# One hand-written step order exchanged for another in a DeltaNet and feed-forward kernel

## The chip, the cores and the metric

The kernel runs on one NeuronCore of one Trainium2 chip. Five engines work from queues of their own: TensorE (PE; its weight loads are shown as PEld), VectorE (DVE), ScalarE (ACT), GpSimd (POOL) and SyncE (SP, which here only issues DMAs). Each executes its own instructions in order, and semaphores tie the queues together. Matrix products are written to PSUM, everything else lies in SBUF. The metric is the device time of one launch in microseconds, the median of a few runs. A profiled execution has its own time and its own span, from the first instruction to the last.

## The reference

Two parts, one after the other. The first is a delta rule over 768 time steps, for 4 batches and 8 heads of size 48; the second is a feed-forward block on its 3072 output rows.

```python
k_n = k / (norm(k) + 1e-6)
for t in range(S):
    y[t] = q[t] @ state
    v_old = state.T @ k_n[t]
    state = state + beta[t] * outer(k_n[t], v[t] - v_old)
x = y as (3072, 384)
out = ((x @ w1) * (x @ w2)) @ w3 @ w_out
```

The weights arrive as float64, w1 and w2 as 384 x 1024, w3 as 1024 x 1024, w_out as 1024 x 384.

## The kernel before, in words

The sequence is cut into 12 chunks of 64 time steps. Inside a chunk the recurrence becomes small matrix products and the inverse of a triangular matrix; the state goes from chunk to chunk. Two chunks at a time share one inverse (V0 to V5) and one block of the feed-forward part (512 columns, u = 0 to 5). The product w3 @ w_out is folded into one matrix at the start.

Every piece of work is a Python generator that emits some instructions between two `yield`s. The string `ORDER` (line 39) names generators; a name's next occurrence runs the generator to its next `yield`. Each engine executes its instructions in the order in which the string emitted them (`in_text_order`, at the end). So the string is the whole schedule: it sets which PE phase follows which, and what stands ahead of what on DVE, ACT, POOL and SP. The framework adds semaphores where data or buffers demand them. Buffers rotate in the order of the calls: two PSUM tiles `ps_w` for the small phases (one while V0 or V1 holds the other), four `ps_f` banks, five `raw` tiles for arriving weights.

The names, with the PE lines that tell them in the profile:

- `k`, `q`, `v`, `p`: loads of a chunk (`p` is the permuted load, 8 DMAs for k and 8 for q; chunks 0 and 1 use `K`, `Q`, PE transposes of L337, instead). `d`: four DVE transposes of what `p` loaded.
- `g`, `N`: squares (POOL), sums (DVE) and the inverse norms of two chunks (14 DVE operations), each with a small PE exchange (L255).
- `P0` to `P35`: a piece of a weight: DMA on SP, two ACT operations (L710, L713), one DVE (L715), one POOL (L717). 0 to 7 are w_out, 8 to 23 w3, 24 to 29 w1, 30 to 35 w2. `t`: transposes of w3 (L752). `f`: half a fold twice (L761), then its copy (L768). `T`: four sums of the folded weight (POOL).
- `s`: scores of a chunk, two PE phases (L367, L373), evacuated by DVE (L379, L397; ACT and POOL for the first two chunks). `u`: four DMAs that store the score blocks in DRAM.
- `V`: the substitution: a load of the blocks (L426), 31 pairs of DVE operations (L440, L445), a store (L453). `V0` and `V1` work in PSUM, with ACT copies ahead (L434) and behind (L449).
- `e`: joins the inverse of a chunk: eight DMAs, one DVE transpose (L481), two PE phases (L498) with an ACT copy after each (L514, L525).
- `n`: two POOL products on v. `c`: the chunk's chain, up to three PE phases (L551): the old values from the state (DVE R, L585), the new values X (L597), the next state S (L616, L618).
- `y`: the chunk's output, one PE phase of 128 matmul records (64 for chunk 0) with a drain between two modes (L655), eight ACT copies to `xT` (L676), and six DMAs.
- `a`, `b`: x @ w1 and x @ w2 for 128 columns, each 6 matmul records (L781), with an ACT copy (L793) and a DVE product (L797). `a25` is block 2, columns of group 5; `b` is the first half of block 0. `S`: 16 POOL sums of their results (L848). `o`: seven PE phases of 16 records against the folded weight (L876). `x`: the output sums (ACT, DVE) and their stores.

The text calls `a`, `b`, `o` and `f` phases dense (full 128 x 128 tiles), the others small.

## Time and profile before

| | us |
|---|---|
| median of 3 runs | 606.77 (606.45 to 607.84) |
| profiled execution | 609.02 |
| its span, first to last instruction | 607.2 |
| PE busy in the span | 554.8 |
| mean granted TensorE clock | 0.943 of full speed |

The page shows one profiled execution. Its second part cuts the span into 40 slices of some 15 us; a digit is the busy share in tenths, PEclk the granted TensorE clock in tenths. The chain of waits goes back from the last instruction to what released it at each step; "issue" is time in which an engine waited for nothing that the profile shows. The busy time by stretch gives, per engine, busy us and the number of instructions, then the granted clock, the DMA share and the rate. A matmul of float32 stands in the trace as two records, each with its weight load.

### The profile page before, as it was taken

What the parts mean: (1) busy time and instruction counts of PE and PEld (TensorE: products, weight loads), DVE (VectorE), ACT (ScalarE), POOL (GpSimd) and SP (SyncE); (2) the same over time, 40 slices, a digit from 0 to 9 for tenths busy, and PEclk for the clock granted to TensorE, in tenths of its full rate; (3) what the DMA queues carried; (4) which work ended last, traced back from release to release, by engine and by line L of the source; (5) the groups of instructions that cost most, each with busy time, mean ns of one, the idle gap of its engine ahead of it and who ended that gap; (6) DMA issues with size and microseconds to landing.
All of it is one profiled execution on the core that took longest, in us unless ns stands there. A gap on an engine that the chain in (4) does not pass through costs nothing.

```text
span 607.2 us, 18976 instructions
## 1 busy us (share of the span) xinstructions
PE 554.8 (91%) x8188; PEld 387.3 (64%) x8188; DVE 334.0 (55%) x792; ACT 159.2 (26%) x333; POOL 175.2 (29%) x223
## 2 busy tenths in 40 slices
PE   4558997869998999999899998999899999999997
PEld 4444655658887864469844587644687446874477
DVE  2551886538975369665597555793464863310112
...
PEclk9657999759999999999899999999899999999999
...
GB/s 193 172 225 271 202 78 164 152 131 143 144 111 72 98 90 100 87 89 76 56 105 74 98 60 77 104 114 79 27 46 78 45 71 18 17 41 13 1 0 52
DMA packets 219506, 57.30 MB, mean 94 GB/s; under 512 B 206656, under 2 KB 212800, under 8 KB 219424
## 3 DMA queue, kind: packets, MB, share of 16 engines
...
q8 instruction: 64, 1.05, 0.8%
q14 instruction: 18, 0.15, 0.1%
...
## 4 chain that ended last, share of the span: by engine, by line
PE 83%; issue 6%; DVE 4%; ACT 3%; DMA 2%; POOL 1%; ACTq 0%; SPq 0%; DVEq 0%; POOLq 0%
PE ps_f L781 41%; PE ps_f L876 19%; PE ps_w L551 5%; PE ps_f L761 5%; PE ps_w L655 4%; PE ps_w L498 2%; PE ps_w L367 2%; PE ps_w L373 2%; PE ps_f L752 1%; DMA ktok<-in_k_dram 1%; PE ps_w L876 1%; POOL w L717 1%; DMA raw<-in_moe_w_out_dram 1%; ACT raw L713 1%; DMA TT<-Vd 1%
## 5 line engine op out<-in xcount | busy, mean ns | idle before, releaser
L781 PE MATMUL ps_f<-xT,w2s 128*128 128x512 f32 (+1 forms) x336 | 131.5, 536 | 0.3 <-issue 0.3
L781 PE MATMUL ps_f<-xT,w1s 128*128 128x512 f32 (+1 forms) x336 | 130.1, 537 | 0.0
L848 POOL TENSOR_TENSOR ab<-ab 128x256 f32<-128x256 f32 x96 | 67.0, 728 | 192.1 <-DVE ab L797 181.9
L781 PEld LDWEIGHTS ps_f<-xT,w1s 128*128 128x128 f32 x336 | 64.4, 193 | 55.7 <-issue 51.2
L781 PEld LDWEIGHTS ps_f<-xT,w2s 128*128 128x128 f32 x336 | 62.6, 190 | 55.7 <-issue 52.2
L793 ACT COPY ab<-ps_f 128x512 f32<-128x512 f32 (+1 forms) x56 | 28.6, 524 | 178.1 <-PE ps_f L781 178.1
L876 PE MATMUL ps_f<-w,ab 128*128 128x192 f32 x376 | 68.6, 336 | 1.2 <-issue 0.7
L797 DVE TENSOR_TENSOR ab<-ab,ps_f 128x512 f32<-128x512 f32 (+1 forms) x56 | 33.4, 604 | 64.2 <-PE ps_f L781 64.1
L876 PEld LDWEIGHTS ps_f<-w,ab 128*128 128x128 f32 x376 | 62.5, 194 | 4.5 <-issue 3.4
L676 ACT COPY xT<-ps_w 48x256 f32<-48x256 f32 x96 | 30.5, 365 | 84.2 <-PE ps_w L655 83.7
L876 PE MATMUL ps_f<-room,ab 128*128 128x192 f32 x272 | 50.4, 339 | 1.1 <-DVE room L907 0.8
L761 PE MATMUL ps_f<-w2s,w3T 128*128 128x384 f32 x128 | 46.7, 523 | 1.7 <-ACT w3T L755 1.7
L445 DVE TENSOR_TENSOR Vb<-Vb,tb 128x31 f32<-128x31 f32 (+15 forms) x124 | 45.0, 363 | 4.3
L440 DVE TENSOR_TENSOR tb<-Vb,Ub 128x31 f32<-128x31 f32 (+15 forms) x124 | 44.4, 358 | 5.2 <-DMA Ub<-Ud 1.6
L876 PEld LDWEIGHTS ps_f<-room,ab 128*128 128x128 f32 x272 | 45.6, 196 | 2.4 <-issue 1.6
L270 POOL TENSOR_TENSOR sq<-ktok 128x384 f32<-128x384 f32 x24 | 19.9, 844 | 78.3 <-DMA qperm<-in_q_dram 29.8
L537 POOL TENSOR_TENSOR vtok<-vtok,n 128x384 f32<-128x384 f32 x24 | 20.0, 849 | 65.3 <-DMA vtok<-in_v_dram 30.3
L761 PEld LDWEIGHTS ps_f<-w2s,w3T 128*128 128x128 f32 x128 | 25.7, 206 | 19.8 <-issue 3.3
L379 DVE TENSOR_TENSOR U<-ps_w,wt 128x512 f32<-128x512 f32 x24 | 16.5, 689 | 36.2 <-PE ps_w L373 36.1
L367 PE MATMUL ps_w<-KQ 48*64 48x128 f32 x384 | 30.2, 302 | 6.7 <-DVE KQ L349 4.3
L717 POOL TENSOR_TENSOR w<-w,raw 128x512 uint32<-128x512 uint32 x16 | 20.9, 1316 | 43.9 <-ACT raw L713 15.4
L373 PE MATMUL ps_w<-KQ 48*64 48x64 f32 x768 | 31.3, 239 | 1.6 <-issue 1.6
...
## 6 DMA issues: line engine op xcount, KB each, us to landing
...
```

The lines of the kernel that those rows point to most:

```text
L367: pe.matmul(ps[half(z), 0, n : n + 128], lhsT=x[:, 0, :], rhs=x.rearrange("p j t -> p (j t)"), start=True, stop=True,)
L373: pe.matmul(ps[half(z ^ j), 1, n + C * j : n + C * j + C], lhsT=x[:, 0, :], rhs=x[:, j, :], start=True, stop=True,)
L440: dve.tensor_tensor(out=tv, in0=V[:, 0 : s + 1, s : s + 1].to_broadcast([P, s + 1, n]), in1=U[:, s, s + 1 : BS].unsqueeze(1).to_broadcast( ...
L445: dve.tensor_tensor(out=o, in0=o, in1=tv, op=ALU.subtract)
L551: pe.matmul(out(ps, r, h, z), lhsT=lhs(r, h, z), rhs=rhs(r, h, z), start=True, stop=True,)
L676: act.copy(out=xT[f, p:NP:2, b : b + NR, cc, :].rearrange("p a r t -> p r a t"), in_=pyv[f, z, b : b + NR],)
L761: pe.matmul(ps[:, 0:DM], lhsT=w3Ts[jc, kc // 4][:, kc % 4 * P : kc % 4 * P + P], rhs=wo[:, kc], start=(kc == 0), stop=(kc == KF - 1),)
L781: pe.matmul(ps[:].rearrange("p b c t -> p b (c t)"), lhsT=w[:, m, js], rhs=x[:, m, :, c0:c1].rearrange("p b c t -> p b (c t)"), start=(m = ...
L793: act.copy(out=t, in_=ps)
L797: dve.tensor_tensor(out=t, in0=t, in1=ps, op=ALU.mult)
L848: pool.tensor_tensor(out=o_, in0=x_, in1=y_, op=op)
L876: pe.matmul(ps[b][:, b, :], lhsT=abs_[u, HF * f + i][:, t0 : t0 + P], rhs=ws_[w][:, i], start=first and i == 0 and (b == 0 or n == "F"), s ...
```

## The change

Only the string `ORDER` is replaced. Both strings hold 1317 entries, and each name occurs equally often in both, so every instruction is the same; their order on each engine differs, and with it the rotation of the buffers. In the PE order the new string puts dense phases (`o`, `a`, `b`) at other places between the small ones. Around chunks 7 to 9, for example, PE goes from

```
before: ... c7 o2 c7 y7 o2 c8 o2 a31 ...   a37 e9 y8 o3 s10 s10 o3 c8 e9 o3 s11 s11 c9 o3 c9 y9 o3 c9
after:  ... c7 o2 y7 o2 c7 o2 a33 ...      a36 y8 s10 o3 e9 s10 o3 c8 e9 o3 c9 s11 s11 c9 o3 y9 o3 c9
```

The diff, cut: the start, and the rows around chunks 4 to 5 and 7 to 9.

```diff
-V0 beta q1 beta beta k0 K0 K0 K0 K0 K0 Q1 g0 g0 q0 Q1 Q1 k1 g0 g0 K1 K1 Q1 K1 Q1 g0 g0 g0 g0 g0
-g0 N0 K1 P10 P10 K1 s1 N0 P10 P13 Q0 P13 P9 P10 t2 P13 P13 P0 P9 P0 N0 P9 P12 P12 P12 P12 P0 P0
-p2 P9 t1 Q0 Q0 d2 P15 d2 k2 P11 t5 Q0 Q0 P15 s0 P15 P15 s0 s0 s1 s1 s0 s0 s0 s1 s1 s1 g1 t7 g1
-g1 g1 P11 P11 P11 P8 P8 P8 P8 P14 P14 P14 P18 P18 P18 t1 t2 t4 P14 t6 P18 t5 P4 P4 P3 P3 P3 t10
-P1 P3 s0 P4 P4 P1 P1 P1 t6 t7 t3 t4 P2 P2 u0 P2 P2 t0 t0 f2 P5 P5 P5 P6 P6 P6 P6 t10 f0 u1 P5 P7
-P7 P7 P7 f2 f2 P19 t3 f1 f1 V0 P19 P19 P19 V0 V0 V0 V0 V0 V0 V0 V0 V0 V0 V0 s1 s1 f0 P17 t11 f3
-t11 f3 v0 V0 P17 P17 P17 P20 P20 f0 V0 V0 t9 P20 P20 f1 t12 t12 V0 V0 V0 V0 P16 P16 V0 V0 P16
-P22 P22 P22 f3 P22 t9 f5 f5 t14 P16 t8 t8 f4 f4 V0 V0 p2 d2 f5 t14 f7 V0 d2 P23 P23 V0 V0 V0 V0
-V0 V0 V0 V0 V0 V0 V0 V0 P23 P23 t15 t15 f4 k3 g1 g1 g1 g1 g1 g1 N1 p3 d3 P21 P21 P21 n0 f6 p3 f7
-f7 V0 P31 e0 e0 P21 N1 N1 e0 P31 P31 P31 s2 e0 n0 t13 e0 e0 d3 t13 P25 s2 s2 c0 c0 P25 P25 s2 s2
-s2 e1 s0 y0 y0 P24 c0 f6 v1 n1 P25 e1 V1 n1 e1 e1 P32 P24 c0 d3 d3 s3 s3 s3 s3 s3 s3 c1 c1 P26
-u2 e1 e1 c1 P26 P26 P30 P26 f6 P30 P30 P30 c1 y1 y0 u3 P32 P32 y1 P24 P28 V1 c1 c1 V1 V1 V1 V1
-P32 V1 V1 V1 V1 V1 V1 P24 b1 b0 b2 b2 b1 V1 V1 P34 b0 b0 b3 b3 b0 V1 y1 a02 P28 P28 a02 a02 a00
-P33 P33 a02 V1 P27 V1 V1 a01 a00 P28 P27 P27 P27 a01 a01 c2 a00 V1 V1 P29 P29 P29 P29 V1 V1 b5
-a05 a01 P34 P34 P34 a03 a00 V1 V1 V1 V1 p4 a06 V1 P33 b5 P33 a03 P35 P35 P35 a05 b7 V1 V1 V1 b7
-b4 b4 a06 P35 V1 a03 V1 V1 V1 V1 v2 n2 n2 b6 b6 a03 k5 k4 g2 b6 b6 c2 d4 d4 g2 p4 g2 a05 a05 g2
-a06 V1 g2 a07 V1 V1 d4 d4 a07 b2 b2 a04 a04 T a06 b3 g2 b3 b1 b1 g2 g2 T a04 a07 T e2 e2 a04 g2
-a07 v3 n3 T e3 e2 e2 b7 e2 s4 e2 c2 n3 g2 N2 s4 b5 s4 s4 b4 c2 s4 y2 y2 b4 s4 p5 p5 c2 c2 o0 b5
...
-g3 d6 g3 N2 g3 N3 e4 a16 p7 c4 c4 s6 s6 e5 s6 a17 v6 n6 y4 s6 s6 s6 a16 y4 o1 e5 x1 e5 e5 S1 c4
-a17 o1 S1 S1 d7 d7 u6 d7 d7 s7 S1 S1 S1 S1 S1 S1 n6 n5 n5 c4 s7 s7 s7 s7 u7 s7 o1 x1 x1 S1 S1 S1
-S1 e5 e5 c5 o1 V3 c5 c5 c5 V3 V3 V3 o1 c5 p8 y5 y5 y5 x1 o1 V3 V3 V3 V3 c5 c6 x1 x1 S1 o1 x1 V3
...
-o2 S2 S2 S2 c6 x2 S2 s9 s9 s9 s9 s9 s9 v8 u9 o2 S2 S2 n7 V4 n7 e7 e7 c7 o2 x2 n8 n8 c7 c7 c7 x2
-V4 o2 V4 V4 V4 V4 c7 c7 V4 V4 y7 o2 c8 x2 c8 S2 V4 S2 v9 o2 x2 y7 y7 a31 k11 x2 x2 x2 S2 S2 V4
...
-g5 c8 a37 c8 g5 N5 a36 S3 d10 d10 e9 e9 a37 S3 y8 y8 o3 S3 S3 S3 S3 s10 x3 p11 d11 s10 s10 V5
-s10 o3 S3 S3 S3 S3 s10 s10 d11 p11 u10 c8 e9 e9 d11 d11 c8 o3 S3 S3 S3 S3 x3 x3 s11 s11 s11 s11
-s11 u11 c9 o3 s11 n9 c9 c9 c9 y9 o3 x3 c9 V5 V5 V5 V5 V5 V5 o3 y9 y9 a44 x3 x3 o3 x3 a44 x3 x3
...
+V0 beta k0 q0 beta beta K0 K0 K0 P14 P14 K0 Q0 g0 k1 g0 g0 g0 g0 g0 g0 g0 g0 g0 Q0 P14 Q0 K0 Q0
+Q0 K1 P9 s0 P9 P14 N0 N0 P9 K1 K1 K1 K1 q1 Q1 N0 P9 t1 P10 P10 P10 P10 P15 P15 t2 Q1 Q1 Q1 t6 Q1
+P11 P11 P15 s1 P15 t7 P8 P8 P11 P8 P11 P8 s0 P13 s0 P13 s0 s0 s1 P18 P18 P18 t1 t2 t3 t0 P12 P12
+t3 P0 s1 t7 t6 P18 t10 P13 P13 t5 P0 P12 P12 s1 s1 t5 P0 P0 t0 p2 d2 t4 P1 s0 s0 P1 P1 s1 d2 P3
+P2 P1 P2 P2 P2 P3 P3 P6 P3 f0 P6 P4 P6 P6 u0 t10 u1 P5 f1 f3 P7 V0 V0 s1 s1 P4 P4 P5 P5 P4 P5 P7
+P7 P7 f0 f0 t4 f3 V0 V0 V0 f1 f2 f2 V0 V0 V0 k2 g1 V0 V0 f3 V0 V0 P22 P22 P16 v0 n0 P16 V0 V0
+P19 P19 P22 P22 t14 f1 V0 V0 V0 V0 P19 P19 t11 V0 V0 V0 P16 f2 t14 t11 V0 V0 V0 f5 P16 n0 P17 f5
+V0 P17 P17 V0 t8 V0 V0 P17 t9 P23 P23 P23 P23 t8 f4 V0 V0 V0 V0 P20 V0 V0 P20 P20 P20 f5 t9 t15
+f4 f7 p3 d3 d3 P21 P21 P21 P21 V0 V0 t12 p2 f4 d2 d2 t15 f7 P25 t12 f6 V0 k3 e0 e0 e0 e0 g1 g1
+g1 g1 g1 g1 g1 g1 g1 N1 f7 e0 e0 t13 t13 v1 P25 P25 P25 s2 N1 c0 N1 s2 s2 s2 c0 P29 s0 y0 P29 s2
+s2 c0 c0 y0 f6 e1 e1 c1 e1 n1 n1 c1 e1 e1 P24 P24 p3 d3 d3 s3 e1 c1 P29 V1 P29 P30 P30 P30 P26
+P26 P31 P31 s3 s3 s3 f6 u2 P32 P32 P30 P24 P24 y0 c1 y1 y1 s3 s3 u3 P26 P26 b3 b3 P31 b1 b1 P32
+P32 P31 c1 c1 P27 b1 V1 V1 b1 P27 P27 P27 V1 V1 V1 V1 b2 b2 b0 b0 b0 V1 V1 y1 a00 a02 V1 c2 b0
+P28 V1 P28 P28 P28 b4 b4 a00 V1 V1 V1 V1 V1 b6 k4 g2 P35 P35 P34 b6 V1 V1 V1 V1 a02 P34 b7 b7
+a02 a02 P33 V1 V1 p4 P33 P34 a05 a03 a03 V1 V1 V1 V1 V1 V1 P34 b5 b5 a07 a05 a04 a04 k5 V1 V1
+P35 a07 P35 a01 a01 a01 V1 V1 V1 V1 v2 V1 p4 a01 V1 V1 V1 e2 a06 a06 P33 P33 a03 g2 a03 a00 a00
+g2 g2 d4 g2 b3 b3 a07 d4 d4 g2 g2 a04 a07 a04 p5 a06 b4 a05 a06 g2 g2 n2 n2 c2 e2 e2 e2 b2 g2
+a05 e2 T T V2 d4 b4 b6 v3 n3 e2 c2 b7 s4 N2 c2 y2 y2 e3 s4 b5 b7 s4 s4 b6 b2 o0 s4 x0 s4 c2 e3
+S0 e3 T e3 p5 T b5 o0 c2 e3 S0 S0 S0 d5 u4 S0 d5 S0 d5 c3 d5 n3 c3 o0 e3 s5 s5 S0 s5 p6 s5 o0 s5
...
+e4 e5 s6 e4 g3 N3 s6 s6 a13 a13 a14 c4 N3 N2 a13 p7 a14 S1 S1 S1 S1 n5 o1 v6 x1 N2 c4 y4 p7 d7
+d7 d7 e5 p8 o1 y4 e5 e5 c4 c4 N3 o1 e5 d7 p8 S1 S1 S1 c5 s6 o1 s6 s6 S1 S1 S1 S1 S1 u6 n5 c5 s7
+s7 x1 s7 s7 S1 S1 s7 s7 x1 c5 o1 c5 c5 y5 n6 x1 o1 y5 c5 c6 u7 V3 y5 V3 V3 x1 x1 S1 S1 o1 x1 x1
...
+a26 e6 c6 g4 s8 a25 a25 n7 N4 N4 c6 y6 y6 v8 s8 s8 o2 a25 a26 S2 S2 S2 S2 S2 c6 S2 e7 e7 S2 p9
+o2 d9 S2 S2 S2 d9 S2 c6 c7 e7 e7 c7 N4 p9 d9 x2 o2 S2 S2 s8 S2 e7 S2 d9 s9 o2 s9 v9 n9 V4 n9 s8
+u8 s8 s9 s9 c7 s9 s9 x2 o2 c7 y7 x2 x2 o2 u9 x2 x2 V4 V4 c7 o2 y7 y7 a33 a33 V4 V4 x2 x2 x2 V4
...
+d10 a30 a30 a33 k11 a35 g5 g5 a35 a35 e8 e8 e8 e8 p11 c8 a33 e9 S3 a32 e8 a37 g5 a35 e8 S3 g5 g5
+g5 d10 c8 c8 c8 a36 y8 y8 e9 g5 a32 s10 o3 p11 e9 e9 N5 a37 s10 V5 s10 s10 d11 a36 o3 S3 s10 s10
+c8 d11 d11 d11 S3 S3 S3 e9 S3 S3 S3 x3 o3 u10 e9 c8 c9 c9 s11 s11 s11 s11 s11 s11 S3 c9 S3 o3 x3
+c9 y9 x3 o3 x3 u11 V5 V5 V5 V5 y9 V5 c9 V5 V5 V5 y9 S3 o3 a45 x3 x3 S3 S3 S3 S3 o3 x3 V5 x3 x3
```

More of the change, by code (lines that the diff above doesn't have):

```diff
@@ L58 @@
-c3 e3 e3 b7 o0 d5 d5 p6 x0 S0 c3 S0 u4 S0 e3 e3 e3 S0 d5 d5 s5 o0 x0 S0 S0 S0 V2 c3 s5 S0 s5 s5
-s5 c3 v4 S0 u5 s5 o0 o0 x0 V2 c3 y3 S0 S0 y3 n4 x0 S0 o0 c3 y3 S0 S0 S0 S0 x0 x0 x0 V2 V2 c4 V2
-V2 p6 x0 V2 o0 V2 x0 x0 x0 a14 a14 a14 V2 V2 V2 V2 V2 a14 V2 V2 V2 a15 a17 V2 V2 a17 V2 V2 V2 V2
-V2 a15 a15 V2 k6 V2 k7 V2 a13 a15 a11 a11 a13 V2 V2 V2 V2 V2 V2 a10 V2 a12 a12 a10 a10 d6 a10 S1
-d6 d6 a13 a13 v5 g3 g3 g3 n4 g3 c4 V2 a12 a12 g3 e4 g3 a11 e4 e4 N2 a11 S1 e4 a16 a16 e4 p7 g3
-g3 d6 g3 N2 g3 N3 e4 a16 p7 c4 c4 s6 s6 e5 s6 a17 v6 n6 y4 s6 s6 s6 a16 y4 o1 e5 x1 e5 e5 S1 c4
@@ L64 @@
-a17 o1 S1 S1 d7 d7 u6 d7 d7 s7 S1 S1 S1 S1 S1 S1 n6 n5 n5 c4 s7 s7 s7 s7 u7 s7 o1 x1 x1 S1 S1 S1
-S1 e5 e5 c5 o1 V3 c5 c5 c5 V3 V3 V3 o1 c5 p8 y5 y5 y5 x1 o1 V3 V3 V3 V3 c5 c6 x1 x1 S1 o1 x1 V3
-V3 x1 V3 V3 V3 a20 a20 k8 x1 x1 x1 a22 a22 c6 a23 a23 a25 a25 V3 V3 V3 V3 V3 V3 V3 V3 V3 V3 V3
-V3 a21 V3 k9 V3 V3 V3 V3 V3 V3 V3 a21 a26 a26 a26 a26 a25 a25 a23 a23 g4 p8 g4 g4 g4 g4 d8 d8
-a24 a22 a24 a24 g4 g4 V3 d8 g4 d8 a22 e6 e6 g4 e6 e6 g4 N4 N3 V4 a24 a20 p9 p9 e7 s8 e6 e6 a21
-v7 s8 s8 s8 s8 c6 s8 a20 S2 e7 u8 a27 a27 N3 c6 y6 a27 d9 d9 d9 d9 e7 a21 y6 S2 a27 S2 S2 c6 e7
@@ L70 @@
-o2 S2 S2 S2 c6 x2 S2 s9 s9 s9 s9 s9 s9 v8 u9 o2 S2 S2 n7 V4 n7 e7 e7 c7 o2 x2 n8 n8 c7 c7 c7 x2
-V4 o2 V4 V4 V4 V4 c7 c7 V4 V4 y7 o2 c8 x2 c8 S2 V4 S2 v9 o2 x2 y7 y7 a31 k11 x2 x2 x2 S2 S2 V4
-S2 S2 p10 o2 V4 V4 v11 x2 x2 x2 a31 V4 V4 V4 V4 V4 V4 d10 V4 a37 a30 V4 V4 V4 V4 V4 a30 V4 a37
-a33 V4 a33 V4 V4 k10 g5 g5 a36 p10 a36 V4 V4 V4 a34 a33 a33 a32 V4 V4 g5 g5 g5 g5 a31 a31 g5 g5
-a34 a34 e8 a32 a34 e8 a35 a35 a35 a32 a35 d10 n9 e8 a30 N4 N4 a30 S3 S3 a32 e8 e8 e9 e8 e9 a36
-g5 c8 a37 c8 g5 N5 a36 S3 d10 d10 e9 e9 a37 S3 y8 y8 o3 S3 S3 S3 S3 s10 x3 p11 d11 s10 s10 V5
@@ L76 @@
-s10 o3 S3 S3 S3 S3 s10 s10 d11 p11 u10 c8 e9 e9 d11 d11 c8 o3 S3 S3 S3 S3 x3 x3 s11 s11 s11 s11
-s11 u11 c9 o3 s11 n9 c9 c9 c9 y9 o3 x3 c9 V5 V5 V5 V5 V5 V5 o3 y9 y9 a44 x3 x3 o3 x3 a44 x3 x3
-V5 V5 V5 V5 x3 a40 a40 x3 a43 a46 a43 a46 a42 a42 a42 V5 V5 V5 V5 n11 n11 V5 V5 V5 V5 V5 V5 V5
-V5 V5 V5 V5 V5 V5 V5 V5 a42 a40 a45 V5 V5 V5 a40 a45 a41 a41 a44 a44 a43 a43 v10 a46 n10 a47 V5
-e10 c9 e10 e10 e10 a41 a41 N5 a46 c10 N5 e10 o4 a47 n10 c10 e10 c10 a45 c10 y10 y10 a47 c10 e11
-e11 e11 a45 a47 e11 o4 c10 c11 c11 e11 x4 o4 e11 c11 x4 x4 S4 S4 S4 S4 o4 S4 S4 S4 S4 S4 S4 S4
@@ L82 @@
-c11 y11 o4 x4 S4 o4 x4 y11 S4 S4 S4 S4 x4 y11 a52 a52 x4 x4 x4 o4 x4 a56 a56 a55 a57 a55 a57 a55
-a55 a54 a54 a52 a52 x4 a54 a50 a50 a50 a54 a50 S5 a51 a56 a56 a51 a51 a51 S5 S5 a57 a53 a57 a53
-a53 a53 S5 o5 S5 S5 S5 S5 x5 o5 S5 S5 S5 S5 o5 S5 S5 S5 S5 x5 o5 x5 o5 x5 o5 x5 x5 x5 o5 x5 x5
-x5 x5 x5 x5 x5
+V0 beta k0 q0 beta beta K0 K0 K0 P14 P14 K0 Q0 g0 k1 g0 g0 g0 g0 g0 g0 g0 g0 g0 Q0 P14 Q0 K0 Q0
+Q0 K1 P9 s0 P9 P14 N0 N0 P9 K1 K1 K1 K1 q1 Q1 N0 P9 t1 P10 P10 P10 P10 P15 P15 t2 Q1 Q1 Q1 t6 Q1
@@ new lines @@
+a02 a02 P33 V1 V1 p4 P33 P34 a05 a03 a03 V1 V1 V1 V1 V1 V1 P34 b5 b5 a07 a05 a04 a04 k5 V1 V1
[3 more added lines that the diff above has]
+S0 e3 T e3 p5 T b5 o0 c2 e3 S0 S0 S0 d5 u4 S0 d5 S0 d5 c3 d5 n3 c3 o0 e3 s5 s5 S0 s5 p6 s5 o0 s5
+s5 p6 c3 k6 u5 x0 S0 o0 x0 v4 c3 y3 c3 y3 S0 S0 S0 S0 x0 o0 S0 S0 S0 S0 c3 c4 n4 x0 n4 x0 o0 V2
@@ new lines @@
+V2 y3 a14 V2 V2 V2 x0 x0 x0 a14 V2 V2 V2 V2 V2 x0 V2 V2 a12 k7 a12 a11 d6 V2 V2 a11 V2 v5 c4 V2
+V2 V2 V2 V2 V2 V2 V2 V2 V2 x0 a17 a17 a17 a17 a15 a16 a15 V2 a10 a15 a10 a10 V2 V2 V2 V2 V2 V2
+V2 a16 a11 a11 a15 e4 a10 g3 g3 e5 a12 a12 V3 e4 g3 g3 g3 d6 d6 a16 d6 a16 e4 a13 g3 g3 g3 g3 e4
+e4 e5 s6 e4 g3 N3 s6 s6 a13 a13 a14 c4 N3 N2 a13 p7 a14 S1 S1 S1 S1 n5 o1 v6 x1 N2 c4 y4 p7 d7
+d7 d7 e5 p8 o1 y4 e5 e5 c4 c4 N3 o1 e5 d7 p8 S1 S1 S1 c5 s6 o1 s6 s6 S1 S1 S1 S1 S1 u6 n5 c5 s7
+s7 x1 s7 s7 S1 S1 s7 s7 x1 c5 o1 c5 c5 y5 n6 x1 o1 y5 c5 c6 u7 V3 y5 V3 V3 x1 x1 S1 S1 o1 x1 x1
@@ new lines @@
+x1 a22 a22 V3 V3 V3 V3 V3 V3 V3 V3 a23 a23 x1 x1 a24 V3 a24 V3 a21 a21 V3 V3 V3 V3 V3 V3 V3 V3
+V3 V3 V3 a24 V3 a24 V3 V3 V3 V3 d8 a20 k8 g4 a20 a20 k9 V3 a27 V3 V3 V3 a22 a27 g4 a21 g4 g4 g4
+a20 g4 g4 e6 S2 a27 a22 n6 g4 a23 a25 e7 a21 e6 e6 g4 a27 v7 n7 c6 e6 a26 a23 d8 d8 d8 a26 e6
+a26 e6 c6 g4 s8 a25 a25 n7 N4 N4 c6 y6 y6 v8 s8 s8 o2 a25 a26 S2 S2 S2 S2 S2 c6 S2 e7 e7 S2 p9
+o2 d9 S2 S2 S2 d9 S2 c6 c7 e7 e7 c7 N4 p9 d9 x2 o2 S2 S2 s8 S2 e7 S2 d9 s9 o2 s9 v9 n9 V4 n9 s8
+u8 s8 s9 s9 c7 s9 s9 x2 o2 c7 y7 x2 x2 o2 u9 x2 x2 V4 V4 c7 o2 y7 y7 a33 a33 V4 V4 x2 x2 x2 V4
@@ new lines @@
+V4 V4 V4 V4 V4 a34 x2 a34 V4 V4 V4 V4 V4 V4 V4 k10 V4 V4 V4 V4 V4 a31 a31 a31 a31 V4 x2 V4 V4 V4
+n8 a30 a30 n8 a36 a36 V4 V4 V4 V4 V4 a37 p10 a37 p10 V4 a32 a32 d10 a34 d10 g5 g5 g5 a34 V4 c7
+d10 a30 a30 a33 k11 a35 g5 g5 a35 a35 e8 e8 e8 e8 p11 c8 a33 e9 S3 a32 e8 a37 g5 a35 e8 S3 g5 g5
+g5 d10 c8 c8 c8 a36 y8 y8 e9 g5 a32 s10 o3 p11 e9 e9 N5 a37 s10 V5 s10 s10 d11 a36 o3 S3 s10 s10
+c8 d11 d11 d11 S3 S3 S3 e9 S3 S3 S3 x3 o3 u10 e9 c8 c9 c9 s11 s11 s11 s11 s11 s11 S3 c9 S3 o3 x3
+c9 y9 x3 o3 x3 u11 V5 V5 V5 V5 y9 V5 c9 V5 V5 V5 y9 S3 o3 a45 x3 x3 S3 S3 S3 S3 o3 x3 V5 x3 x3
@@ new lines @@
+a45 a45 x3 V5 V5 V5 x3 V5 V5 V5 a45 a40 a40 V5 a46 a46 a42 V5 V5 V5 V5 V5 V5 a42 a42 a42 V5 a44
+V5 a44 a44 V5 V5 v11 V5 V5 V5 V5 V5 a41 V5 a41 a41 a44 v10 n10 a43 V5 a43 a41 a43 e10 a40 N5 e10
+e10 e11 e10 a47 a47 c9 e10 a43 n10 e11 c10 c10 a40 S4 a47 e10 c10 o4 S4 N5 x4 c10 c10 c10 y10
+y10 a47 a46 e11 a46 o4 e11 e11 c11 S4 S4 e11 o4 S4 n11 n11 c11 c11 o4 S4 S4 x4 S4 S4 c11 y11 S4
+o4 S4 y11 x4 x4 S4 o4 y11 a57 S4 S4 a57 x4 x4 x4 x4 S4 S4 o4 x4 x4 a56 a56 a56 a56 a50 a50 a50
+a54 a54 x4 a54 a50 a54 a55 a55 a55 a55 a51 a51 a51 a52 a52 a51 a53 a53 a53 a53 a52 a57 a52 o5
@@ L86 @@
+a57 S5 S5 S5 S5 S5 S5 S5 S5 o5 S5 S5 S5 S5 x5 o5 S5 S5 o5 o5 o5 S5 S5 x5 x5 x5 x5 x5 x5 x5 x5 x5
+o5 x5 x5 x5 x5
 """
```

## The prediction

> **What bounds the kernel now.** I read the page first (busy shares, the 40 slices, the chain), then busy time by stretch, then the chain in order of time around the stretches that stood out, and last each engine's timeline up to 180 us.

> ```profile
> PE 554.8 (91%) x8188; PEld 387.3 (64%) x8188; DVE 334.0 (55%) x792; ACT 159.2 (26%) x333; POOL 175.2 (29%) x223
> PE   4558997869998999999899998999899999999997
> PEclk9657999759999999999899999999899999999999
> ...
> q8 instruction: 64, 1.05, 0.8%
> ...
> PE 83%; issue 6%; DVE 4%; ACT 3%; DMA 2%; POOL 1%; ACTq 0%; SPq 0%; DVEq 0%; POOLq 0%
> ```

> TensorE bounds it, and its work is not changed. What can change is its idle time and its clock: low in slices 1 to 4 and 7 to 9, and dented in slices 19 and 28.

> ```profile
> core 0: us, PE busy (x) PEld busy (x) DVE busy (x) ACT busy (x) POOL busy (x), PEclk, DMA share, GB/s
> 110.00:134.00 24.00, 18.39 (x588) 14.68 (x592) 9.69 (x15) 10.21 (x23) 8.96 (x9) 0.64 0.70 145
> ...
> 291.00:302.00 11.00, 8.89 (x268) 8.21 (x258) 6.67 (x18) 2.54 (x8) 0.00 (x0) 0.84 0.24 37
> ...
> 371.00:376.00 5.00, 2.83 (x170) 2.34 (x172) 4.65 (x13) 0.00 (x0) 0.00 (x0) 1.00 0.35 63
> ...
> 431.00:440.00 9.00, 7.40 (x182) 6.72 (x177) 4.21 (x10) 4.15 (x11) 3.75 (x6) 0.81 0.32 43
> ```

> These stretches lose time between stretches where PE is busy nearly throughout. The chain of waits inside them:

> ```profile
> 290.77 0.86 PE ps_w L551 x64
> 291.63 1.34 PE ps_w L655 x96
> ...
> 293.51 1.74 issue
> 295.25 0.55 PE ps_w L655 x22
> 295.80 4.47 PE ps_f L876 x16
> ...
> 301.58 2.84 PE ps_f L876 x16
> ```

> ```profile
> 371.27 0.86 PE ps_w L551 x64
> ...
> 373.37 2.05 issue
> ...
> 376.53 2.80 PE ps_f L876 x16
> ```

> ```profile
> 433.06 1.49 issue
> 434.54 0.33 PE ps_w L655 x7
> 434.87 4.48 PE ps_f L876 x16
> ```

> Each stall lies in an output step (y5, y7, y8; L655) that follows another small phase at once; "issue" says that no semaphore held it. Queue q8 brings 64 packets of 16 KB. PE has 8188 matmuls and 8188 weight loads, 256 for each packet. Counted along the trace, the three stalls fall at PE instructions 8642, 11202 and 12482, apart by 10 and 5 times 256. So PE's program comes in blocks of 256, and a stall waits for one. From entering a block to having the next took 4.06, 3.95 and 3.85 us here. A block of two small phases lasts some 2.2 us (y 2.27 us for 256 instructions, c phases 0.86 to 1.08 for 128, e 0.69 for 128, s 1.06 for 96); one that also holds an L876 product (2.80 us for 32) or an L781 product (2.58 for 12) lasts over 4. The 4.47 after the first stall, against 2.84, is the low clock.

> **The sum's basis.** The profiled execution took 609.02 (span 607.2 and 1.8 around it), 2.25 over the median of 606.77. Differences are worked out in its span and taken from the median.

> **The steady part, from e2's first product on (176 us).** I counted the new list in blocks of 256 (two records for a matmul, the 165 semaphores and drains spread as now, so a boundary is known to some 30 instructions).
> - y7 gets a dense product before it, and so does y8: the stalls go. y7 took 4.57 against 2.34 for an undisturbed y: -2.23. y8 took 4.07: -1.73, and the low clock on the product behind it (4.55 against 2.87) goes: -1.68.
> - y9 (3.76, 0.33 of it issue and 1.03 the X evacuation, L597) also gets a product before it: -1.42. c9's first phase no longer waits for chunk 11's scores: -0.56.
> - y5 still follows c5's last phase at once, with a boundary inside: its 1.74 and 1.66 stay.
> - e5's first product now follows y4 at once and a block starts there: 2.31 us long, 2.9 with the sequencer's lead. I take +1.3; between 0 (boundary elsewhere) and +3.4 (as y5, clock included), nearest to the plain stalls.
> - e5's second product waits for an ACT copy (L514) that now stands behind y4's eight xT copies (8 x 365 ns), with only a 2.80 product as cover: +0.7 (0 to 1.5).
> - s7, s7, c5 and s11, s11, c9 now follow each other; with two ps_w banks the third waits for evacuations of 0.69 and 0.61: +0.5 each (0 to 1).
> - The substitution on VectorE (V, 62 operations, 23.5 us without its guests) feeds e: V's end to e's first product took 10.5 us. e4, e6 and e10 start 0.7 to 1.8 us after their input is ready now. u7, u9 and u11 come later against PE (scores 7 move from before e5's second product to just before c5's second), and PE's work from the last scores to e8 and e10 is 46.1 and 49.0 us against chains (u's store, V's load, V, 10.5) of some 46 and 48: +0.3 each (0 to 2).
> - Hidden: e5's DMAs pass p7's sixteen on SP and gain 8 us nobody waits for. Two of the four weight sums (T, 2 us each, POOL) now stand behind n3 and one slab sum, which wait for v3's DMAs; o0's second product needs them some 4 us later than they end. Without that cover its queue would stop for the difference. Other k, p, v, n, g steps move by less than the tens of us between landing and use.
> Sum: -7.6 + 1.3 + 0.7 + 1.0 + 0.6 = -4.0.

> **The start (up to e2).** Here DMA bounds the weights, then VectorE bounds V0, then waits bound the small phases.
> - Piece 14 goes ahead of k1 on SP (0.5 MB, some +2.6 us for K1 and the norms), and p2's eight DMAs and k2 go from 9th and 11th place to after the 12th piece and after V0's load: 0.4 MB less ahead of U's store. V0's copies (L434) wait on ACT behind the fourth fold half instead of the third. These oppose each other: V0's start, 62.4 now, I leave there (-2 to +3).
> - V0's guests on VectorE: two transposes fewer (0.65 each), one piece more (0.43): -0.9.
> - k3's four DMAs (0.63 each) move between V0's store and e0's eight; the store lands 3.1 us after issue (89.8 to 92.9), which covers their 2.5. Without it e0 is late by 2.5.
> - g1's four reductions and the 14 operations of N1 (3.4 us) now stand on VectorE between e0's transpose and c0's X. From the transpose to y0's end took 11.2; I add up 12.5: +1.3 (0 to +3).
> - From y0 to y1's end took 23.85, with issue stalls of 0.80, 2.43 and 0.70 at a clock of 0.64. The new order puts c1 ahead of e1 and spreads scores 3; its longest chain (fold half 2.74 to 4.55, c1, e1, two ACT steps, P30's conversion, two evacuations, X, y1) adds to some 19.5: -4.4 (-8 to 0).
> - Piece 28 now waits on SP behind y1's six xT DMAs (0.6 each), and b4 stands some 2.4 us for it. That lies inside the next wait: V1 starts earlier with y1 and still sets e2's first product, from y1's end 43.2 against 42.7: +0.5 (0 to +3).
> Sum: -0.9 + 1.3 - 4.4 + 0.5 = -3.5.

> Together -7.5: **599.3 us**.

> [...]

> **Rivals.**
> - R1, slower: V0 starts late. Its copies wait for the fold half that needs the last w_out pieces, and the norms of chunk pair 1 stand in c0's way. For: K1 and the first norms are later, and four fold halves at half clock from 49 us end at 62.4. Against: less DMA traffic ahead. Price: +5 for the start, +3 for g1 and N1, against -4.4 and -1 left of the rest: 609.4. It decides from a first V0 product after 66 us.
> - R2: the steady stalls only change places, since every 256th instruction has its boundary somewhere: steady -0.5, start -3.5: 602.8. For: the count is good to 30 instructions. Against: y7, y8 and y9 are now 2 to 3 us of dense work away from the last small phase.
> - R3: the V chain becomes the bound in the steady part; e6, e8 and e10 wait, and what the stalls gave is idle there: steady -1.5: 601.8. For: 0.7 to 1.8 us of room. Against: the new list has fewer guests between V and e8.
> - R4: y5 and e5 lose nothing (boundaries fall in dense work) and the start gains its full bound: about -13: 593.8.
> - R5: nothing measurable. A list of the same steps at a 91% busy PE; 606.8.
> [...]

> **Chances.** Forecast 0.35 (its own range 596 to 602), R2 0.18, R4 0.15, R1 0.16, R3 0.10, R5 0.06. A measurement of this kernel tells about 0.2% from none (1.2 us). Faster 0.78, same 0.06, slower 0.16. The range 593.0 to 608.0 leaves out half of R1's side and the far end of R4.

> **What the profile after would show.** No issue stall over 1 us in y7, y8, y9, and the products behind them at 2.8; a stall at y4 to e5 and still one at y5. V0's first product near 62, y1's end near 128 to 130 (133.5 now), e2's first product near 172 (176.2). Wrong would be: V0 after 66, a hole ahead of c0 or b4 beyond 3 us, e8 or e10 waiting over 2 us, or new stalls in c and s phases.

## The result and the profile after

The new list is slower: 614.29 us (median of 7, 610.73 to 620.51) against 606.54 for the old one on the same chip (7 runs, 605.42 to 607.97). The ratio is 1.0106, with a 95% interval of 1.0072 to 1.0139. On a second chip, beside the kernels below, it was 1.0086 (1.0053 to 1.0120). Forecast were 599.3 us, a range of 593.0 to 608.0, and "faster".

The profiled execution of the new list took 610.73, the shortest of its seven; that of the old one had taken 609.02, above its median. So the two profiles differ by 1.7 us where the medians differ by 7.7, and no profile shows the whole loss. The page of the new list, with its busy times, the slices of PE and its clock, and the shares of the chain that ended last:

```profile
PE 553.8 (91%) x8188; PEld 384.8 (63%) x8188; DVE 334.7 (55%) x792; ACT 159.5 (26%) x333; POOL 175.3 (29%) x223
...
PE   4679797788998989998899999999999999999997
...
PEclk9859899779999989998899999999999999999999
...
PE 63%; SPq 11%; DMA 9%; DVE 6%; ACT 5%; issue 3%; POOL 1%; POOLq 0%; ACTq 0%; DVEq 0%
```

PE's work and share are as before. But only 63% of the chain is PE now (83% before): SP's queue and DMA landings have taken 20% (2% before). The clock has its dents in slices 15, 19 and 20, counted from 0 (before in 19 and 28). Busy time of the new list by stretch:

```profile
core 0: us, PE busy (x) PEld busy (x) DVE busy (x) ACT busy (x) POOL busy (x), PEclk, DMA share, GB/s
110.00:134.00 24.00, 16.62 (x492) 14.21 (x484) 8.11 (x15) 11.81 (x24) 7.75 (x6) 0.64 0.61 135
214.00:228.00 14.00, 11.41 (x99) 7.22 (x98) 7.96 (x23) 0.92 (x3) 2.46 (x3) 0.88 0.53 126
271.00:283.00 12.00, 10.26 (x345) 9.31 (x345) 2.48 (x4) 5.35 (x13) 7.42 (x11) 0.86 0.37 45
296.00:313.00 17.00, 13.99 (x297) 11.91 (x296) 8.83 (x23) 2.54 (x8) 0.00 (x0) 0.90 0.33 84
376.00:391.00 15.00, 13.82 (x354) 12.69 (x351) 6.57 (x18) 2.54 (x8) 1.74 (x3) 1.00 0.44 101
431.00:440.00 9.00, 8.88 (x258) 6.09 (x257) 6.19 (x23) 1.62 (x6) 0.00 (x0) 1.00 0.39 49
```

The last two rows are y7 and y8: their long stalls are gone and the clock is full. The second, third and fourth rows, at clocks of 0.88, 0.86 and 0.90, lose time instead. The second was no place of loss before at all. The chain of waits there, in order of time (start, length, what):

```profile
214.62 0.54 SPq L426
...
217.16 4.52 DMA xT<-xT
...
221.72 4.54 PE ps_f L781 x6
```

The first product of block 1, `a14`, waits for one of y3's xT transfers, which takes 4.52 us behind V2's load (L426), and then runs 4.54 us instead of 2.8. In the third row y4 and e5 follow each other:

```profile
273.40 0.67 PE ps_w L655 x32
274.07 0.51 PE ps_w L498 x44
274.58 1.62 issue
276.20 0.26 PE ps_w L498 x7
276.46 4.48 PE ps_f L876 x16
```

Again a stall for the program and a slow product behind it.

PE ends o0's, o1's, o3's and o5's last products with the same work done in both lists (four small records apart at o1). So their ends, read from the traces, cut each execution into four comparable stretches (us; the kernels below are named in the experiments):

| profile of | to the end of o0 | o0 to o1 | o1 to o3 | o3 to o5 |
|---|---|---|---|---|
| before | 221.59 | 82.83 | 167.45 | 131.27 |
| new list | 219.38 | 91.73 | 162.11 | 131.35 |
| new list again | 215.17 | 96.25 | 162.36 | 131.05 |
| new start, old rest | 218.06 | 86.96 | 166.99 | 131.26 |
| new middle alone | 219.83 | 90.18 | 166.42 | 131.26 |
| one wait removed | 220.30 | 91.56 | 162.40 | 131.58 |
| all causes moved | 221.32 | 86.38 | 162.31 | 131.31 |
| and two sums | 219.03 | 81.33 | 162.59 | 131.65 |

The new list wins 2 to 6 at the start and 5 between o1 and o3, and loses 9 to 13 between o0 and o1.

### The profile page after: what moved, and what is told of

Its sections match the earlier page's. It is cut to its first block, busy times and chain, and to the rows that moved or that the text cites. A ratio compares the mean times of both kernels' runs of the same rounds, so it can differ in the third digit from the quotient of the medians.

```text
span 608.6 us, 19000 instructions
## 1 busy us (share of the span) xinstructions
PE 553.8 (91%) x8188; PEld 384.8 (63%) x8188; DVE 334.7 (55%) x792; ACT 159.5 (26%) x333; POOL 175.3 (29%) x223
## 3 DMA queue, kind: packets, MB, share of 16 engines
q8 instruction: 64, 1.05, 0.8%
## 4 chain that ended last, share of the span: by engine, by line
PE 63%; SPq 11%; DMA 9%; DVE 6%; ACT 5%; issue 3%; POOL 1%; POOLq 0%; ACTq 0%; DVEq 0%
PE ps_f L781 37%; PE ps_f L876 14%; SPq L230 4%; PE ps_w L551 3%; PE ps_f L761 3%; PE ps_w L655 2%; DMA raw<-in_moe_w_dram 2%; PE ps_w L498 2%; DVE tb L440 2%; DVE ps_w L445 2%; SPq L462 1%; DMA X<-in_q_dram 1%; SPq L414 1%; SPq L702 1%; SPq L469 1%
## 5 line engine op out<-in xcount | busy, mean ns | idle before, releaser
L781 PE MATMUL ps_f<-xT,w1s 128*128 128x512 f32 (+1 forms) x336 | 133.8, 548 | 6.4 <-ACT xT L676 2.7
L781 PE MATMUL ps_f<-xT,w2s 128*128 128x512 f32 (+1 forms) x336 | 131.3, 536 | 1.5 <-ACT ab L793 1.5
L781 PEld LDWEIGHTS ps_f<-xT,w1s 128*128 128x128 f32 x336 | 65.3, 197 | 64.6 <-issue 54.6
L781 PEld LDWEIGHTS ps_f<-xT,w2s 128*128 128x128 f32 x336 | 62.6, 190 | 58.2 <-issue 51.7
L876 PE MATMUL ps_f<-w,ab 128*128 128x192 f32 x376 | 67.2, 331 | 2.2 <-DVE osb L907 1.8
L876 PEld LDWEIGHTS ps_f<-w,ab 128*128 128x128 f32 x376 | 60.7, 190 | 5.4 <-issue 4.6
L876 PE MATMUL ps_f<-room,ab 128*128 128x192 f32 x272 | 51.5, 345 | 1.4 <-DVE room L907 0.8
L876 PEld LDWEIGHTS ps_f<-room,ab 128*128 128x128 f32 x272 | 46.7, 200 | 2.7 <-issue 1.8
L761 PE MATMUL ps_f<-w2s,w3T 128*128 128x384 f32 x128 | 45.1, 508 | 1.0 <-POOL w2s L717 0.8
L618 DVE TENSOR_TENSOR S<-S,ps_w 48x768 f32<-48x768 f32 x20 | 19.0, 950 | 24.7 <-PE ps_w L551 24.5
L907 DVE TENSOR_TENSOR room<-room,ps_f 128x384 f32<-128x384 f32 (+1 forms) x13 | 7.0, 537 | 40.8 <-PE ps_f L876 40.7
```

Source lines behind the costliest of these rows:

```text
L761: pe.matmul(ps[:, 0:DM], lhsT=w3Ts[jc, kc // 4][:, kc % 4 * P : kc % 4 * P + P], rhs=wo[:, kc], start=(kc == 0), stop=(kc == KF - 1),)
L781: pe.matmul(ps[:].rearrange("p b c t -> p b (c t)"), lhsT=w[:, m, js], rhs=x[:, m, :, c0:c1].rearrange("p b c t -> p b (c t)"), start=(m = ...
L876: pe.matmul(ps[b][:, b, :], lhsT=abs_[u, HF * f + i][:, t0 : t0 + P], rhs=ws_[w][:, i], start=first and i == 0 and (b == 0 or n == "F"), s ...
```

## The experiments

In the diffs, a line shows the string around a move, and the rest of it is unchanged.

**1. Which part of the list.** Four kernels join parts of the two lists: entries of one up to a product, then what is left in the order of the other.

```diff
+h1_new_start:  new list to o0's last product | rest old
+h2_new_tail:   old list to o2's last product | rest new
+h3_new_middle: old to o0's last product | new to o1's last | rest old
+h4_old_middle: new to o0's last product | old to o1's last | rest new
```

> The new list up to the end of o0's last product (some 219 us), then what is left in the order of the old list. Theory A (the loss lies in the middle): in the profiled executions the new list has done everything up to o0's last product 2.2 us earlier than the old one (219.38 against 221.59 us) and loses the lead after it; so this kernel is faster than before by about 2.2: 604.3, as steady as before. Theory B (the loss lies in the start, and the profiled execution is a lucky one): the new list's times run from 610.7 to 616.2 while the old one's lie within 2.5, the chain of waits of its profile now goes through SP's queue and DMA landings, and most DMA traffic is in the start; then this kernel is slower than before, 608 to 612, and its times scatter over 4 us or more.

> The old list up to the end of o2's last product (some 388 us), then what is left in the order of the new list: y8 and y9 get dense products before them, nothing else of the change is in it but the end. Theory A: the stalls of y8 and y9 go and nothing replaces them. Between o2's and o3's last products the old list lost 6.0 us to idle time and low clock, the new one 1.55: 4.4 us faster than before, 602.1. Rival (the stalls only change places): 606, no change.

> The old list up to o0's last product, the new one from there to o1's last product, then what is left in the order of the old list. Theory A: between these two products the old list lost 4.3 us to idle time and low clock and the new one 13.0 (a14 waits for an xT load, e5 and y5 stall, each with a slow product behind it, and o1's last product waits); all of this is made in the middle itself: 8.7 slower than before, 615.2. Rival C: the wait at a14 is inherited from the start, where V2's load and y3's DMAs were put; then the old start takes it away with its slow product, some 4 of the 8.7, and this kernel takes 611.

> The new list up to o0's last product, the old order from there to o1's last product, then what is left in the order of the new list. Theory A: the start's -2.2 and the -4.4 of y8 and y9 stay, y7 gets its product (its stall of 2.05 goes, of which the new list gave 0.5 to 1.2 back) and the middle's +8.7 is gone: 599 to 600, faster than both. Theory B (the loss is in the start): 604 to 609 with a wide scatter.

Measured against before: new start 1.0003 (0.9971 to 1.0034), new tail 0.9979 (0.9954 to 1.0004), new middle 1.0127 (1.0086 to 1.0169), old middle between new ends 1.0063 (1.0032 to 1.0093). The middle alone makes a loss as large as the whole. h1's start is 3.5 us early, and in its profile `a14` then waits 2.62 us and runs 4.54: the start is not the loss, as theory B had it, but its lead does not last, and theory A's 604.3 did not come either. h2 came out between its two theories and cannot be told from no change. In h3 `a14` does not wait, so that wait comes with the start, as rival C had it; the middle still costs 7.7 us without it, by four stalls: 1.02 at e5, 1.78 at c4, 2.02 at s7, 2.15 at y5 (the last was there before, with 1.74). h4 missed theory A and lies at the upper end of theory B, which h1 speaks against: where its two orders meet, `a23` waits 2.38 us for one of x1's sums, which waits for an output store. Neither list has such a wait, so h4 says little.

**2. Single causes, first try.** g1 takes the loads ahead of V2's load away from the new list. g2 moves one product in the old list from behind y5 to ahead of it, g3 does so at y5, y7, y8 and y9, g4 puts g3's order behind the new start with g1's moves. In g2, g3 and g4 the moved product adds to its bank before x1's first sum has read it, so block 1's outputs differ; the amount of work is the same.

```diff
 g1_dma
-s5 p6 c3 k6 u5 x0 ... x0 v4 ... c4 n4 x0 n4 x0 o0 V2 V2 y3 a14 V2 V2 V2 x0 x0 x0 a14
+s5 c3 u5 x0 ... x0 ... c4 x0 x0 o0 V2 V2 y3 p6 k6 v4 n4 n4 a14 V2 V2 V2 x0 x0 x0 a14
 g2_y5
-o1 c5 p8 y5 y5 y5 x1 o1 V3
+o1 c5 p8 o1 y5 y5 y5 x1 V3
```

> The new list with five entries moved: q's permuted load of chunk 6 (eight DMAs), chunk 6's k, chunk 4's v and the two products that read it go from ahead of V2's load on SP to behind y3's xT DMAs. Theory A (a transfer waits behind a transfer): V2's 0.5 MB load is issued some 5 us earlier, has landed when y3's six xT DMAs are issued at 215, these land 2 us later instead of 6, and a14 waits no longer: its wait of 2.35 and its slow 4.54 against 2.81 go, 4.1 us less than the new list: a ratio to before near 1.004, 608. Rival C (the wait only moves): V2's chain or the scores behind it set e4 some microseconds later anyway; the ratio stays at 1.010, and e4's first product waits for the inverse by what a14 waited.

> The old list with one entry moved: o1's sixth product goes from behind y5's matmuls to ahead of them. Theory A (the stall waits for a block of the program, and a block that holds a dense product is long enough): the block that ends inside y5 grows from 2.15 us to 4.6 us of work, the stall of 1.74 goes and with it the low clock on the product behind (4.47 against 2.80), 3.4 us less: 602.4 against 605.8 of before. Rival D (stalls change places): the next boundary stalls instead, no change. Rival E (the inverse becomes the bound): V3, e6's input, depends on scores that lie ahead of y5; e6 starts 0.7 to 1.8 us after its input is ready in the old list, so only that much is left of the gain: 604 to 605, and e6's first product or the work ahead of it waits.

> The old list with four entries moved: each of the products that follow y5, y7, y8 and y9 at once goes ahead of that y (o1's sixth, o2's fifth, o3's first and fifth). Theory A: all four stalls go with their low clocks, 3.4 + 2.0 + 3.2 + 1.4 = 10.0 less: 595.8. Rival E (the inverse becomes the bound): what y8 gave stays (its scores s10 and s11 come after it), of the other three only the room that e6, e8 and e10 have is left, some 1.2 each: 3.2 + 3.6 = 6.8 less, 599. Rival D (stalls change places): 604 to 606.

> The new list up to y3's xT DMAs with the five entries moved behind them, then what is left in the old order with the four moves of the products. Theory A: the start's 3.5 (the profile of the new start with the old rest: 218.06 against 221.59 us at o0's last product) is no longer lost at a14, and the four stalls are gone: 605.8 - 3.5 - 10.0 = 592.3. Rival E: with the inverse as the bound between, 596 to 599. Rival B (the start's lead holds in some executions only): no better than the four moves alone.

Measured: 1.0126 (1.0088 to 1.0163), 1.0056 (1.0021 to 1.0091), 1.0144 (1.0101 to 1.0187), 1.0117 (1.0084 to 1.0151). All four are slower. g1 came nearest to rival C, and g4 is no better than g3, as its rival B had it; g2 and g3 lie outside all their theories. The profiles say why. In g1 `a14` starts without a wait, but block 0's output stores now stand behind the fourteen loads on SP. The chain of g1 behind them:

```profile
228.89 3.08 DMA out_dram<-osb
...
232.09 0.56 DVE osb L907
...
232.70 5.54 PE ps_f L781 x7
```

A sum waits for its output buffer, and `a11` 7.41 us for that sum's bank. The wait was moved, not removed. In g2 the stall inside y5 is gone, and c6's first phase waits for the state instead (chain of g2):

```profile
298.94 0.97 DVE S L618
...
300.04 1.28 PE ps_w L551 x64
301.32 4.29 PE ps_f L876 x16
```

PE stood 2.81 us for it, with a slow product behind. So the product behind y5 had a use: it covered the update of c5's state. Likewise in g3 the product behind y7 had covered y7's xT transfers (`a31` waits 2.26) and that behind y8 the copies that free its bank (s10 waits 1.76). g4 has the same three waits (2.80, 2.20 and 1.76). By this reading a y with two covers needs two products, one on each side; the new list has that at y7.

**3. One cause each.** f1 moves chunk 8's loads in the new list, f2 puts products between its small phases, f3 takes only y8 and y9 from the new list, with a cut that leaves no seam, and f4 mends g2.

```diff
 f1_p8
-d7 e5 p8 o1 y4 e5 e5 ... o1 e5 d7 p8 S1 ... a23 a23 x1 x1 a24
+d7 e5 o1 y4 e5 e5 ... o1 e5 d7 S1 ... a23 a23 x1 x1 p8 p8 a24
 f2_o1
-y4 p7 d7 d7 d7 e5 p8 o1 y4 e5 e5 c4 c4 N3 o1 e5 ... c5 s6 o1 s6 s6
+y4 p7 d7 d7 d7 o1 e5 p8 y4 e5 c4 c4 N3 o1 e5 e5 ... c5 o1 s6 s6 s6
 f3_y8y9
+old list to e9's transpose | rest new
 f4_y5
-o1 c5 p8 y5 y5 y5 x1 o1 V3 V3 V3 V3 c5 c6
+o1 c5 c5 p8 x1 o1 y5 y5 y5 V3 V3 V3 V3 c6
```

> The new list with two entries moved: both halves of chunk 8's permuted load (sixteen DMAs), which stand between y4 and o1's third product, go behind the last of block 1's output sums. Theory F (the program's blocks come late because loads stand before them): in the profiles with the new middle, block fetches between y4 and y5 begin 2.4 to 4.9 us after PE has entered the block before, against about 1 us where the DMA engines are idle, and these loads run then. Without them the stalls at e5, c4 and s7 (1.62 in the profile of the new list; 1.02, 1.78 and 2.02 with the new middle alone) shrink by 1 to 2 each: 3 to 5 us less than the new list, a ratio to before of 1.003 to 1.006. Theory G (only the length of the run of small phases counts): no change, 1.010, and the fetches are as late as before.

> The new list with three phases moved: o1's second product goes between y4 and e5's first product, e5's second product behind o1's third, and o1's fourth ahead of the second phase of s6. No load is moved. Theory G (the length of the run of small phases): the block that held y4 and e5 alone (1.86 us of work) now holds a product, the stall of 1.62 and the slow product behind it (4.55 against 2.84) go, 3.3 us less than the new list, a ratio of 1.005; where other executions lose at c4 and s7 too, up to 5. Theory F: the loads make the fetches late anyway; a block of 2.8 us (s6, s7, s7) stalls in their place, and the ratio stays at 1.009 to 1.011.

> The old list up to the transpose of e9, then what is left in the order of the new one: y8 and y9 with their dense products, without the waits of up to 1.4 us that the earlier cut (at o2's last product) brought at block 3's first columns and at o3's last product. Theory A: 4.4 us less than before, 601.3. Rival E (e10's inverse becomes the bound behind them): 603 to 604.

> The old list with o1's sixth product and the sum that has to precede it (x1's first sum on VectorE) ahead of y5, and the update of chunk 5's state ahead of both, so that c6's first phase finds its state ready (in the kernel that moved the product alone it waited 2.7 us for it). Theory A: the stall of 1.74 and the slow product (4.47 against 2.80) are gone and nothing waits in their place: 3.4 less than before, 602.3. Rival E (the inverse becomes the bound): the lead is lost ahead of e6, 604 to 605.

Measured: 1.0039 (1.0007 to 1.0070), 1.0055 (1.0026 to 1.0083), 0.9997 (0.9970 to 1.0024), 1.0078 (1.0051 to 1.0105). f1 and f2 each take about half of the new list's loss away (1.0106 and 1.0086 on two other chips). In f2's profile nothing stalls at e5 (the product behind y4 runs 2.80); s7 waits 2.35 for chunk 5's old values instead. That is theory G, as far as a base on other chips allows. f1's gain can't be laid on late fetches: its profile still has 1.62 at e5. What is missing there is the wait of 1.07 at o1's last product, which the second profile of the new list below does not have either, and the slow product behind y5 (2.87 against 4.18). Its number is theory F's, but theory F is not shown. f3 missed both its theories: it gives nothing that can be measured, although y8 and y9 are clean in its profile. f4 missed both of its own too. In it the state is ready, and the product waits 2.72 for x1's sum, which now stands behind the state's update on VectorE, then `a20` 2.26 for y5's xT: a third and a fourth wait under one stall.

**4. What adds up.** r4 is the new list again. r1 moves only the loads that can move past the stores, r2 takes all named causes together, r3 has the new start with r1's moves, the old middle and the new end.

```diff
 r1_a14
-s5 p6 c3 k6 u5 x0 ... V2 V2 V2 x0 x0 x0 a14
+s5 c3 u5 x0 ... V2 V2 V2 x0 x0 x0 p6 k6 a14
 r2_all: r1_a14, f1_p8 and f2_o1, and
-n5 o1 v6 x1 ... c5 o1 s6 s6 s6 ... u6 n5 c5 s7
+n5 n5 o1 v6 x1 ... c5 c5 o1 s6 s6 s6 ... u6 s7
 r3_mix
+r1_a14 to block 0's last store | old to e9's transpose | rest new
```

> The new list unchanged, beside the kernels below on one chip: the base for what each of them takes away, and a second profile of it. Theory A (the same four places lose in every execution): the wait at a14, the stalls at e5 and y5 and the wait at o1's last product are in this profile too, and the ratio to before is 1.009 to 1.011. Theory H (each of them comes or stays away from execution to execution): stalls at c4 and s7 as with the new middle alone, or none at e5.

> The new list with two entries moved: the second half of chunk 6's permuted load (eight DMAs) and chunk 6's k (four DMAs) go from ahead of V2's load on SP to behind the second of block 0's output stores, so that they hold up neither V2's load nor y3's xT nor those stores (the kernel that moved five entries ahead of the stores traded the wait at a14 for one of 7.4 us at a11). Theory A: V2's load is issued some 5 us earlier and has landed before the xT DMAs; a14 starts without a wait and at full clock: 4 us less than the new list. Rival C: another wait takes its place ahead of e4, and no more than 1 is left of it.

> The new list with the moves of the kernel before this one, chunk 8's loads behind block 1's sums, a product between y4 and e5's first product and one ahead of the second phase of s6, and chunk 5's last product on v and its old values emitted earlier (s7 waited 2.35 us for them). Theory A (the causes add): the new list's 6.4 less 4 (a14), 2 to 3 (the loads) and 3 (the product at e5): 3 us faster than before, a ratio of 0.995. Rival E (each lead is lost at the next wait on the inverse or on an evacuation): 1.000 to 1.004.

> The new list with chunk 6's loads moved as above up to block 0's last store, the old list from there to the transpose of e9, and the new one from there on. Theory A: the start's 3.5 stays (it was lost at a14 in the kernel with the new start and the old rest, which came out at 1.0003), the middle is the old one, y8 and y9 give 1 to 4: 4.5 to 7.5 less than before, 599 to 602, a ratio of 0.988 to 0.993. Rival E: the lead is lost where the old middle waits for something other than PE; 1.000.

Measured on one chip: the new list 1.0086, r1 1.0022 (0.9988 to 1.0056), r2 0.9934 (0.9905 to 0.9964), r3 0.9950 (0.9920 to 0.9981). So the two entries of r1 carry 0.64%, 3.9 us, as theory A had it (4), though the two intervals still overlap. The gain stands in the medians: r1's own profile is of its slowest execution (611.75 against a median of 608.58), and there `a14` does not wait, but the program's stalls at e5, c4, s7 and y5 (0.94, 1.30, 1.76 and 2.47) fill the stretch up to the 91.56 of the table. r2 is theory A's (the causes add up), and r3 lies between its two. SP's own queue in the profile of the new list, from its timeline (start, length, line, what):

```profile
204.73 1.02 SPq L230 DMA_DIRECT2D qperm<-in_q_dram  x2
205.85 2.82 SPq L202 DMA_DIRECT2D ktok<-in_k_dram  x4
208.76 2.20 SPq L414 DMA_DIRECT2D Ud<-U  x4
211.06 1.98 SPq L893 DMA_DIRECT2D out_dram<-osb  x2
213.14 1.32 SPq L213 DMA_DIRECT2D vtok<-in_v_dram  x2
214.62 0.54 SPq L426 DMA_DIRECT2D Ub<-Ud  x1
215.20 4.40 SPq L687 DMA_DIRECT2D xT<-xT  x6
```

and the same in r1:

```profile
206.01 2.31 SPq L213 DMA_DIRECT2D vtok<-in_v_dram  x2
208.48 0.59 SPq L426 DMA_DIRECT2D Ub<-Ud  x1
212.86 3.75 SPq L687 DMA_DIRECT2D xT<-xT  x6
```

With the new list the load goes out 0.6 us ahead of the transfers and lands at 220.97; the six transfers land from 221.15 to 222.01, every 0.17 us, though the first was issued at 215.20. In r1 the load goes out 4.4 us ahead, and the first transfer lands 1.98 after its issue.

The second profile of the new list shows what the first did not: the chain between y4 and y5.

```profile
272.40 1.15 issue
...
277.76 1.65 issue
...
289.95 2.03 issue
```

These are e5, c4 and s7: h3's stalls, and y5's comes behind them (1.63). In the first profile only e5's and y5's had come. Theory H holds: the same list stalls at different boundaries in different executions.

**5. One wait left.** In r2's profile o1's last product stands behind V3's load by way of VectorE (chain of r2):

```profile
294.91 5.06 DMA Ub<-Ud
...
300.95 0.57 DVE room L907
...
301.54 0.56 DVE osb L907
...
302.25 5.46 PE ps_f L876 x16
```

V3's first operations wait there for the load, and the sum that frees the product's bank stands behind them. r5 puts two sums ahead:

```diff
 r5_sums: r2_all, and
-y5 V3 V3 x1 x1 S1 S1 o1
+y5 x1 x1 V3 V3 S1 S1 o1
```

> The kernel with all the moves, and two more: two of block 1's output sums go ahead of V3's first two operations on VectorE, which stand there until V3's load has landed. In its profile o1's last product waited 2.91 us for one of these sums and ran 5.46 us instead of 2.84. Theory A: this wait and its low clock go, up to 5.6 us less than the kernel with all the moves: a ratio to before between 0.985 and 0.990. Rival E (the inverse becomes the bound): V3 and e6 are no earlier, so the lead is lost ahead of e6, 0.992 to 0.995.

Measured: 600.03 against 607.01, a ratio of 0.9884 (0.9849 to 0.9919). That is theory A's number, though r5 ran on another chip than r2 and their intervals overlap. In its profile the product waits no longer and runs at full clock, and the stretch from o0 to o1 takes 81.33 instead of 86.38:

```profile
296.82 0.55 DVE osb L907
...
297.52 2.84 PE ps_f L876 x16
```

This list is faster than the old one beside it by 1.2%, and the new one was slower than the old one on both chips on which it ran unchanged. It is the new one with eleven entries at other places.

## Why the prediction was wrong, point by point

- **The start: -3.5, right in its sum, by luck.** e2's first product began at 175.4 on average in the 7 profiles with the old start, and at 172.4 in the 12 with the new one: -3.0. Two misses cancel in it. V0's first operation, left where it was, began 4.9 earlier on average (62.4 and 58.2 in the two first profiles). From there to y1's end it was -3.1, forecast -4.0, so that y1 ended 8.0 earlier (averages 124.3 and 132.3). From y1 to e2, forecast +0.5 and bounded by +3, it was +5.0 on average. The new list took 47.98 there in its profile, not 43.2: the first `b3` waited 2.68 for y1's copies, which stood on ACT behind a weight piece, `b4` 1.39 for piece 28, the one wait that had been named, and `a02` 1.47 behind ACT's work on another piece. One of the stalls listed there, 0.70, lies behind y1's end (134.48 against 133.52); no term rests on it.
- **"Hidden: ... Other k, p, v, n, g steps move by less than the tens of us between landing and use" is the step that failed first.** It is true of the moved loads, and beside the point. Chunk 6's loads had moved ahead of u5's store and V2's load on SP; what they delayed was V2's load, and behind it y3's xT. The working asked who waits for the moved step, and not who is queued behind it. In the first profile the wait and its slow product took 4.1 us, in the second 5.9, and moving two entries gave 3.9 back. The lead of the start (2.2 and 6.4 at o0's end in these two profiles) is lost there.
- **e5: +1.3, mis-sized.** It was 1.62 and a product of 4.55 against 2.84: 3.3, the upper bound (+3.4).
- **s7, s7, c5: +0.5, mis-sized.** The term counted evacuations. In the second profile s7 stalls 2.03 for the program, and c4 1.65, which had no term. In h3 the stalls at e5, c4 and s7 are 4.8 of the 7.4 that its stretch from o0 to o1 lost against before, without any wait at `a14`: the mechanism, a block of 256 that runs out, was the prediction's own, but the three places were priced at +1.3, 0 and, for another cause, +0.5.
- **y5's stall: kept, right.** 1.82 (1.74) and 4.18 behind it.
- **y7, y8: the stalls went, as said.** y7 lasted 2.34, and the product behind y8 2.80. But y7's boundary moved into the next product (0.60). And y2, which had no term, now stalls for the program (1.40 and 1.21 in the two profiles), in place of three smaller stalls behind it (0.71, 0.44 and 0.77).
- **The price of y8 and y9 was too high.** All stalls of one profiled execution were subtracted from the median, while that execution lay 2.25 above it. From o2's to o3's last product the old order took 83.50 in it, and 80.47, 80.95, 80.95 and 82.59 in the other four profiles that have this order whole; f3 took 80.22. f3 measured what the two are worth there: 0.2 us, +-1.6. Its stretch from o1 to o3 took 167.22, as before (167.45). So most of the 5 us that the new list wins in this stretch seems to come from what stands ahead of e9's transpose; but r3, with the same y8 and y9, took 164.28, and no run takes the two apart.
- **A wait without a term:** o1's last product behind V3's load. Scores 7 were moved, and the working followed them to e6, where there was room, but not to x1's sums on VectorE. It waited 1.07 in one profile of the new list, not in the other, and 3.02 in r2's; r5's profile shows what its removal gives.
- **e8 and e10: +0.3 each.** They did not wait. R3 was wrong: in the profiles of r1, r2 and r5 no first product of e6, e8 or e10 waits for the inverse.
- **The rivals.** R1 had the sign and not the cause: V0 was early. R2 comes nearest: stalls went to e5, c4 and s7 as they left y7 and y8, one of the signs of being wrong that the prediction named. It was given 0.18, and the wait at `a14` on top was in no rival.
- **What stays open.** Both profiles of the new list are among its fastest executions (610.73 and 611.00 against medians of 614.29 and 612.95). 2 to 3.6 us of its loss stand in no trace. What f1 gains is not divided between late fetches and the sum.
